# A separate issue order for each stage of an attention cycle, with other array halves for its scores

## The chip, the cores and the metric

The kernel runs on one core of one Trainium2 chip. The metric is the device time of one execution in microseconds (us). Three runs of the kernel before took 1853.1, 1853.3 and 1855.0 us; the median is 1853.3.

In the profile PE is TensorE's matmuls, PEld its weight loads, DVE is VectorE, ACT ScalarE, POOL GpSimd and SP the engine that issues most DMAs. Views of single instructions give start and duration in us from the span's start.

## The reference

Two branches work on the same input x of 2048 rows (tokens) by 640 features. A is attention with 32 heads of 20 features; B is a Fourier mixing. A gate per row blends them.

```python
g = sigmoid((x * gate_w).sum(-1, keepdims=True))
# A: q, k, v = x @ wqkv, split into 32 heads of 20
p = softmax(q @ k.T * 20 ** -0.5)          # per head, 2048 x 2048
a = concat_heads(p @ v) @ wo
# B: DFT along the features, then along the rows, real part
ar, ai = x @ hid_re.T, x @ hid_im.T        # 2048 x 640
b = seq_re @ ar - seq_im @ ai              # 2048 x 640
return g * a + (1 - g) * b
```

## The kernel before

**The attention's grain.** The 32 heads are 16 pairs; a pair is worked in two units of 1024 query columns, so there are 32 units. A unit has 32 steps: 16 tiles of 128 keys times 2 groups of 512 queries. One step is two "e" scores, one per head of the pair. An "e" is a matmul of 62 rows by 512 columns into a PSUM bank (line 1076) and an exponential on ScalarE that reads the bank (line 1082).

The maximum that the exponential needs is found ahead of time, by "m" scores: the same products with queries as the stationary side (line 194), each followed by a maximum over 512 columns on VectorE (line 196). They run 43 steps ahead of the "e" scores (LEAD). After a unit's last "m" the maxima are negated, split and turned, and go through DRAM into two more rows of the query operand, so that the later product comes out with the maximum subtracted.

**Array halves.** The two heads of a pair lie on rows 0 to 63 and 64 to 127 of their operands. A score therefore uses one half of the TensorE array, by rows: half 0 or half 1. In a step's two scores z = 0 comes first and z = 1 second, and the table FIRST says which of the two goes to which half: h = z, flipped where the table has a 1. The table has an entry for each of the four steps of a cycle and one row each for "e" and "m". All scores, "e" and "m" alike, take their banks in turn from the same five (`bank()`, line 142).

**The other branch as filler.** Branch B, with its sums of rows and columns combined so that fewer products are needed, is cut into pairs of matmuls: one on half 0 into bank yp0 and one on half 1 into bank yp1, 64 rows by 320 columns each. Pairs come from one long chain of generators: `hid_pair` (line 482, the DFT along the features), `dft_step` (line 779, along the rows) and `out_tile` (line 861, the output projection of finished rows). When a tile's last pair is issued, the reading of yp0 by ScalarE and of yp1 by VectorE is put into `extras`, with the step at which it falls due, and adds and stores are set for later steps.

**A cycle.** Everything is issued in one order written out by hand. A cycle is four steps, and a string says what is issued in it: "e" and "m" are scores, "F" is a place for pairs, and "B" is the burst. In the burst due extras run, and then the attention's second product (`av_step`, line 715; the matmuls of line 721) for the two key tiles whose exponentials are finished. These use all 128 rows, so neither half can work on scores or pairs meanwhile.

```python
ORDER = "emFemFFFFemFeFFmeFFemFFFmmFFmeeB"
LATE = "eeeeFFFFFFeeeEB"
FIRST = {"e": (0, 0, 1, 1), "m": (1, 1, 1, 1)}
```

There are 256 cycles. Cycles 0 to 55 are the hidden stage, with 15 pairs each; 56 to 223 the sequence stage, with 48 pairs in three cycles; 224 to 245 carry output tiles, 12 pairs each, in the same string ORDER; and from 246 on LATE is used. There the "m" scores have run out, and already in cycle 245 none is left. ORDER has 15 places. The list `goals` (lines 984 to 990) spreads a cycle's pairs over its places: with 16 pairs one place gets two, with 12 some places get none.

**What hangs on the order.** `score` (line 1055) issues a score and its reader; the first "e" of a step calls `begin`, which issues the DMAs set for that step, and the second calls `end`. `fill` (line 1000) issues pairs until the place's goal is reached. `burst` (line 1090) runs extras whose step has come. The steps at which extras, stores and loads fall due are counted from `now[0]`, the step whose "e" scores were begun last.

Of the kernel before, what the change touches and what calls it, by code (L numbers as in the profile page):

```python
# [32 lines left out]

ORDER = "emFemFFFFemFeFFmeFFemFFFmmFFmeeB"
LATE = "eeeeFFFFFFeeeEB"
FIRST = {"e": (0, 0, 1, 1), "m": (1, 1, 1, 1)}


LEAD = 43
# [49 lines left out]
def mix_kernel(ctx: ExitStack, tc: tile.TileContext, xa, xh, wqk, wb, wr, cdft, wo, out):  # L91
    nc = tc.nc
    pe, act, dve, pool, sp = nc.tensor, nc.scalar, nc.vector, nc.gpsimd, nc.sync
# [81 lines left out]

    mx, nms, ends = {}, {}, []
    rows_, done_tiles = [], []
    now, later = [-1], {}

    def at_step(i, fn):  # L180
        later.setdefault(i, []).append(fn)
# [302 lines left out]
    def hid_pair(u):  # L484
        n, hf, k = u // 8, u // 4 % 2, u % 4
        _, _, factor, targets = FEATURE[n]
        ps = [new_y(z)[:, :HE] for z in range(2)]
        fresh = [(th, ri, hf, k) not in seen for _, th, ri in targets]
        seen.update((th, ri, hf, k) for _, th, ri in targets)
        rows = [a_scr[ri, hf, th, k] for _, th, ri in targets]  # L490
        olds = []
        for (_, th, ri), new, row in zip(targets, fresh, rows):
            old = None
            if th == ri:
                old = acc(ri, hf, k)
            elif not new:
                old = slots.pop(0)
                slots.append(old)
                at_step(now[0] + 4, functools.partial(sp.dma_start, old, row))
            olds.append(old)  # L500
        done_ = 0
        for d in range(ND):
            for a, b in ((0, 0), (0, 1), (1, 0)):
                for z in range(2):
                    r = slice(64 * z, 64 * z + 64)
                    pe.matmul(ps[z], lefts[n][a][r, d, k * P : k * P + P], rights[2 * n + hf][r, b, d],  # L506
                              start=done_ == 0, stop=done_ == 3 * ND - 1)
                done_ += 1
                if done_ < 3 * ND:
                    yield  # L510
        direct = [i for i, ((_, th, ri), new) in enumerate(zip(targets, fresh)) if new and th == ri]
        m = olds[direct[0]] if direct else raw_tile()[:, : 2 * HE].rearrange("p (s c) -> p s c", s=2)

        def read():
            act.activation(m[:, 0], ps[0], AF.Copy, scale=factor)
            dve.tensor_scalar(m[:, 1], ps[1], factor, 1.0, op0=ALU.mult, op1=ALU.mult)  # L516

        def add(sign, old):
            pool.tensor_tensor(old, old, m, op=ALU.add if sign > 0 else ALU.subtract)  # L519

        extras.append((now[0], read))
        ends_ = {(th, ri): i for i, f in enumerate(FEATURE) for _, th, ri in f[3]}
        for (sign, th, ri), new, row, old in zip(targets, fresh, rows, olds):
            if not new:
                extras.append((now[0] + 3, functools.partial(add, sign, old)))
            if th != ri or ends_[th, ri] == n:
                at_step(now[0] + (4 if new else 11), functools.partial(sp.dma_start, row, m if new else old))
        yield

    step = 0  # L530
# [38 lines left out]
    for s in range(0, NS, 2):  # L569
# [6 lines left out]
        if 4 <= s <= 12:  # L576
            add, finish = make_set(*sets.pop(0), *(pair_tile().rearrange("p z c -> p (z c)")[:, : RW // 2] for _ in range(2)))
# [199 lines left out]
    outs, extras, made = {}, [], {}  # L777

    def dft_step(g):
        n, t, s = g // NS // HT, g // NS % HT, g % NS  # L780
        if s == 0:
            new_y(0), new_y(1)
            outs[n, t] = []
        if s % 8 == 0 and g // 8 + 3 < 2 * UNITS:
            cfin.append(load_c(g // 8 + 3))
        if s % 8 == 4 and cfin and 2 < g // 8 + 2 < 2 * UNITS:
            cfin.pop(0)()
        if s == 8:
            for _, th, hf in PRODUCTS[n][2]:
                tt = th * HT + t  # L790
                y = None
                if (tt, hf) in signs:
                    y = apool[0].tile([P, HE], F32, name="yt", bufs=4)
                    sp.dma_start(y, y_scr[tt, :, hf * HE : (hf + 1) * HE])
                outs[n, t].append(y)
        c = cparts[g // 8]
        cs = slice((s % 8) * P, (s % 8 + 1) * P)
        a = at[n % 2, s]
        for z, (cz, az) in enumerate(((0, 0), (0, 1), (1, 0))):
            for h in range(2):  # L800
                r = slice(64 * h, 64 * h + 64)
                pe.matmul(yp[h][:, :HE], c[r, cz, cs], a[r, az], start=s == 0 and z == 0, stop=s == NS - 1 and z == 2)  # L802
            if z < 2:
                yield
        w = g % (HT * NS) - 16
        if n + 1 == len(PRODUCTS) and w >= 0:
            d, r = divmod(w, 8)
            if r == 0 and d < ND:
                wos[d] = raw_tile()[:, :D]
                sp.dma_start(wos[d], wo[:, d])  # L810
            if r == 5 and d < ND:
                raw = wos.pop(d)
                for h in range(2):
                    wos[d, h] = a_tile(1, 2 * d + h)
                    split(wos[d, h][:, 0], wos[d, h][:, 1], raw[:, h * HE : (h + 1) * HE], pool, pool)
        if s == NS - 1:
            m = apool[0].tile([P, HE], F32, name="m", bufs=3)
            y0, y1 = yp[0][:, :HE], yp[1][:, :HE]

            def read():  # L820
                act.activation(m, y0, AF.Copy)
                dve.tensor_tensor(m, y1, m, op=ALU.add)

            extras.append((now[0], read))
            for out_, y in zip(PRODUCTS[n][2], outs.pop((n, t))):
                extras.append((now[0] + 5, functools.partial(finish_y, out_, t, m, y)))
        yield


# [31 lines left out]
    def out_tile(tt, hf):  # L861
        new_y(0), new_y(1)
        if hf == 0:
            k = tt - PRE[0]
            yo[tt] = f32(a_tile(1, 12 + k) if k < 4 else a_tile(0, k)).rearrange("p z c -> p (z c)")
            assert all(st[tt, h] == 0 for h in range(2))
            sp.dma_start(yo[tt], y_scr[tt])
        o = opre[tt]
        for d in range(ND - 1):
            for z, (oz, wz) in enumerate(((0, 0), (0, 1), (1, 0))):  # L870
                for h in range(2):
                    r = slice(64 * h, 64 * h + 64)
                    pe.matmul(yp[h][:, :HE], o[r, oz, d], wos[d, hf][r, wz], start=d == 0 and z == 0, stop=d == ND - 2 and z == 2)  # L873
                if (d, z) != (ND - 2, 2):
                    yield
        m = apool[0].tile([P, HE], F32, name="m", bufs=3)
        y0, y1 = yp[0][:, :HE], yp[1][:, :HE]
        g = gate[:, tt : tt + 1]

        def read():  # L880
            if now[0] < total - LEAD:
                act.activation(m, y0, AF.Copy, scale=g)
            else:
                dve.tensor_scalar(m, y0, g, 1.0, op0=ALU.mult, op1=ALU.mult)
            dve.scalar_tensor_tensor(m, y1, g, m, op0=ALU.mult, op1=ALU.add)  # L885

        def add():
            y = yo[tt][:, hf * HE : (hf + 1) * HE]
            pool.tensor_scalar(y, y, ngate[:, tt : tt + 1], float(signs[tt, hf]), op0=ALU.mult, op1=ALU.mult)
            pool.tensor_tensor(y, y, m, op=ALU.add)  # L890

        extras.append((now[0], read))
        extras.append((now[0] + 3, add))
        yield

    def finish_y(target, t, m, y):
# [63 lines left out]
    HID = 8 * len(FEATURE)  # L960
# [20 lines left out]
        at_tile += n  # L981
    assert cycles[-1][1] <= last + 1
    late = -(-(total - LEAD) // 4)
    at_goal = 0
    for c0, c1, count in cycles:
        for c in range(c0, c1):
            share = count * (c + 1 - c0) // (c1 - c0) - count * (c - c0) // (c1 - c0)
            places = (LATE if c >= late else ORDER).count("F")
            goals[c] = [at_goal + share * (f + 1) // places for f in range(places)]
            at_goal += share  # L990

# [63 lines left out]
    def score(kind):  # L1055
# [2 lines left out]
        heads[kind] += 1  # L1058
        i, z = divmod(x, 2)
        h = z  # L1060
        if kind == "m" or i <= 4 * late:
            h ^= FIRST[kind][(i - (LEAD if kind == "m" else 0) - 1) % 4]
        if kind == "m":
            s_mm(i, h)()
            if z:
# [44 lines left out]
        else:  # L1110
            score(kind)
    for c in range(total // 4):
        for kind in "e" * (c == late) + (LATE if c >= late else ORDER):
            if kind == "F":
                fill(c)
            elif kind == "B":
                burst(c)
            else:
                score(kind)
# [125 lines left out]
```

## Time and profile before

| | |
|---|---|
| median of three runs | 1853.3 us |
| the profiled execution's own time | 1854.3 us |
| its span, first to last instruction | 1852.5 us |
| mean granted TensorE clock | 0.999 |
| TensorE matmuls in flight | 99% of the span |
| weight loads / VectorE / ScalarE / GpSimd busy | 72% / 79% / 67% / 70% |
| hidden stage, cycles 1 to 55 | 345.6 us |
| sequence stage, 168 cycles | 1063.7 us |
| output stage, 21 cycles with "m" scores | 128.3 us |

A stage's time runs from the start of one burst to the start of another. The time of a cycle is the stage's time over its cycles. In the views that follow, a row of the busy time by stretches gives the stretch, its length, the busy time and number of instructions of each engine, the granted clock, the share of the DMA engines and GB/s. A row of the timeline gives start, duration, engine, line, operation, output and inputs, shape and how many instructions of one kind follow each other, and in brackets the idle time before it with what ended it.

### The profile page before, as it was taken

To read this page: it belongs to the slowest core of one execution; us is meant where nothing else is said; L and a number is where in the kernel's file an instruction comes from. 1 tells how busy PE (TensorE), PEld (TensorE's weight loads), DVE (VectorE), ACT (ScalarE), POOL (GpSimd) and SP (SyncE) were. 2 spreads that over 40 slices of the span, in tenths; PEclk is the share of its full clock that TensorE was granted. 3 is DMA by queue.
4 is the path that set the end of the run, shared out by engine and by line. 5 is a ranking of instruction groups with operands and counts; after the bars stand their busy time and mean duration, and the time that the engine had idled before them with its cause. 6 is when DMAs were issued, how large, how long until landed. Compare 5 with 4: busy or idle time off the path is not lost. (4 is left out here: it accounts for less than half of the span.)

```text
span 1852.5 us, 45906 instructions
## 1 busy us (share of the span) xinstructions
PE 1842.4 (99%) x17917; PEld 1339.8 (72%) x17917; DVE 1460.3 (79%) x2428; ACT 1237.0 (67%) x2378; POOL 1302.6 (70%) x1103
## 2 busy tenths in 40 slices
PE   9999999999999999999999999999999999999998
PEld 8988877677676677677677767767767767766666
DVE  4157489888888888888888888888888888889953
ACT  4233377777777677677766767667676767777785
POOL 1379635666678988556879999867889898734444
PEclk9999999999999999999999999999999999999999
DMA  7899874777666675536577686646585856542224
GB/s 236 203 312 360 291 212 142 224 217 210 222 215 203 193 224 157 145 101 177 184 203 240 171 254 191 199 123 181 156 222 185 233 163 187 154 105 76 64 56 155
DMA packets 195101, 349.63 MB, mean 189 GB/s; under 512 B 54095, under 2 KB 107471, under 8 KB 192835
## 3 DMA queue, kind: packets, MB, share of 16 engines
q1 hardware_dynamic: 193523, 340.63, 61.2%
q0 software_dynamic: 1360, 6.07, 1.5%
q8 instruction: 141, 2.31, 0.5%
q14 instruction: 77, 0.63, 0.1%
HBM read 257.79 MB, written 88.65 MB: 187 GB/s over the span
## 5 line engine op out<-in xcount | busy, mean ns | idle before, releaser
L196 DVE TENSOR_REDUCE mx<-ps 128x1 f32<-128x512 f32 x2048 | 1300.4, 686 | 209.7 <-PE ps L194 190.8
L1082 ACT ACTIVATE p<-ps 128x512 f32<-128x512 f32 x2048 | 1088.1, 598 | 424.5 <-PE ps L194 218.3
L194 PE MATMUL ps<-kst,qst 60*128 60x512 f32 x2048 | 776.5, 413 | 1.1 <-DMA qst<-qk_scr 0.8
L1076 PE MATMUL ps<-qst,kst 62*128 62x512 f32 x2048 | 695.5, 415 | 0.6 <-DMA qst<-m_scr 0.6
L802 PE MATMUL yp<-x,part 64*128 64x320 f32 x5376 | 644.8, 306 | 0.0
L802 PEld LDWEIGHTS yp<-x,part 64*128 64x128 f32 x5376 | 582.5, 186 | 7.6
L1076 PEld LDWEIGHTS ps<-qst,kst 62*128 62x128 f32 x2048 | 332.6, 184 | 223.6 <-DVE mx L196 128.9
L721 PE MATMUL av<-p,v 128*21 128x512 f32 x4096 | 492.5, 596 | 0.0
L194 PEld LDWEIGHTS ps<-kst,qst 60*128 60x128 f32 x2048 | 368.0, 184 | 13.3 <-issue 1.1
L133 POOL TENSOR_TENSOR part<-raw,part 128x1024 fp32r<-128x1024 f32 (+3 forms) x134 | 296.8, 2215 | 10.2
L721 PEld LDWEIGHTS av<-p,v 128*21 128x21 f32 x4096 | 95.3, 100 | 207.4 <-issue 206.5
L132 POOL CAST part<-raw 128x1024 fp32r<-128x1024 f32 (+2 forms) x127 | 125.0, 985 | 129.7 <-PE yp L802 93.3
L667 POOL TENSOR_TENSOR raw<-raw,raw 128x1024 f32<-128x1024 f32 x78 | 188.1, 2412 | 38.6 <-DMA raw<-in_cdft 23.1
L506 PE MATMUL yp<-wb,x 64*128 64x320 f32 x1680 | 207.6, 307 | 0.0
L506 PEld LDWEIGHTS yp<-wb,x 64*128 64x128 f32 x1680 | 179.7, 186 | 3.2 <-DVE x L516 0.2
L519 POOL TENSOR_TENSOR x<-x,raw 128x640 f32<-128x640 f32 x40 | 62.5, 1563 | 44.4 <-DVE raw L516 40.9
L133 POOL TENSOR_TENSOR x<-araw,x 128x320 fp32r<-128x320 f32 x96 | 83.8, 872 | 7.7
L873 PE MATMUL yp<-x,part 64*128 64x320 f32 x720 | 87.2, 308 | 0.0
L890 POOL TENSOR_TENSOR x<-x,m 128x320 f32<-128x320 f32 x30 | 26.2, 873 | 79.1 <-DVE m L885 68.4
L873 PEld LDWEIGHTS yp<-x,part 64*128 64x128 f32 x720 | 75.8, 185 | 2.6
L696 POOL TENSOR_TENSOR araw<-araw 128x320 f32<-128x320 f32 x80 | 69.9, 873 | 1.9 <-DMA araw<-a_scr 1.9
L366 PE MATMUL yp<-x,part 64*128 64x512 f32 x480 | 64.2, 397 | 1.8 <-ACT p L372 1.5
(111 smaller groups left out, 1369.5 us busy)
## 6 DMA issues: line engine op xcount, KB each, us to landing
raw<-in_cdft SPq DMA_DIRECT2D x188, 512.0 KB
araw<-a_scr SPq DMA_DIRECT2D x176, 160.0 KB
qk_scr<-p SPq DMA_DIRECT2D x40, 512.0 KB
w_scr<-wb SPq DMA_DIRECT2D x36, 400.0 KB
wb<-w_scr SPq DMA_DIRECT2D x9, 1600.0 KB
kst<-qk_scr SPq DMA_DIRECT2D x90, 160.0 KB
qst<-qk_scr SPq DMA_DIRECT2D x90, 160.0 KB
part<-in_xh SPq DMA_DIRECT2D x10, 1024.0 KB
```

What stands on the lines that cost most here:

```text
L132: e1.tensor_copy(dst1, src)
L133: e2.tensor_tensor(dst2, src, f32(dst1), op=ALU.subtract)
L194: pe.matmul(ps, q[b : b + KROWS, qt * P : (qt + 1) * P], k[b : b + KROWS, kc * 512 : (kc + 1) * 512], start=True, stop=True)
L196: return lambda: dve.tensor_reduce(mx[n][:, h, qt, kc : kc + 1], ps, axis=AX.X, op=ALU.max)
L506: pe.matmul(ps[z], lefts[n][a][r, d, k * P : k * P + P], rights[2 * n + hf][r, b, d], start=done_ == 0, stop=done_ == 3 * ND - 1)
L667: pool.tensor_tensor(raws[0], raws[0], raws[1], op=ALU.add if PRODUCTS[n][0][1][0] > 0 else ALU.subtract)
L696: pool.tensor_tensor(raws[0], raws[0], raws[1], op=ALU.add if PRODUCTS[n][1][1][0] > 0 else ALU.subtract)
L721: pe.matmul(av[32 * j : 32 * j + DH + 1, :], v[:, kt, h * (DH + 1) : (h + 1) * (DH + 1)], pp[qc][:, h, :], start=kt == 0, stop=kt == NS - 1)
L802: pe.matmul(yp[h][:, :HE], c[r, cz, cs], a[r, az], start=s == 0 and z == 0, stop=s == NS - 1 and z == 2)
L873: pe.matmul(yp[h][:, :HE], o[r, oz, d], wos[d, hf][r, wz], start=d == 0 and z == 0, stop=d == ND - 2 and z == 2)
L1076: pe.matmul(pt, k[b : b + KROWS + 2, kt * P : (kt + 1) * P], q[b : b + KROWS + 2, qc * 512 : (qc + 1) * 512], start=True, stop=True)
L1082: act.activation(pts[n, kt, qc][:, h], pt, AF.Exp, scale=float(DH) ** -0.5)
```

## The change

Each of the three stages gets a string and a pair of half tables of its own. The sequence stage's string has 16 places, the output stage's 12, and the hidden stage's keeps 15, so that each place gets exactly one pair. The number of scores, pairs and bursts in a cycle stays the same. The late stage keeps its string, and its tables hold zeros, which is what its scores had before.

In the new strings the last "F" of a cycle comes after the cycle's last step has begun. The new function `ended` caps the step from which due times are counted at the step before it, so that reads, adds and stores are due at the steps they had.

```diff
-ORDER = "emFemFFFFemFeFFmeFFemFFFmmFFmeeB"
-LATE = "eeeeFFFFFFeeeEB"
-FIRST = {"e": (0, 0, 1, 1), "m": (1, 1, 1, 1)}
+HIDDEN = "emeFFmeFFFmFeFmeFFmFFeFFeFFmemmB", {"e": (0, 1, 1, 1), "m": (1, 0, 1, 0)}
+SEQUENCE = "ememFFeFFFFmeFFmeFmFFFeFFemFFmemB", {"e": (1, 0, 1, 0), "m": (0, 1, 1, 1)}
+OUTPUT = "ememeFFFmFeFmFeFmeFFmFemFFemB", {"e": (1, 0, 0, 0), "m": (0, 0, 1, 1)}
+LATE = "eeeeFFFFFFeeeEB", {"e": (0, 0, 0, 0), "m": (0, 0, 0, 0)}
...
-    now, later = [-1], {}
+    now, at_cycle, later = [-1], [0], {}
+
+    def ended():
+        return min(now[0], 4 * at_cycle[0] + 3)
...
-        extras.append((now[0], read))
+        extras.append((ended(), read))
...
-                extras.append((now[0] + 3, functools.partial(add, sign, old)))
+                extras.append((ended() + 3, functools.partial(add, sign, old)))
             if th != ri or ends_[th, ri] == n:
-                at_step(now[0] + (4 if new else 11), functools.partial(sp.dma_start, row, m if new else old))
+                at_step(ended() + (4 if new else 11), functools.partial(sp.dma_start, row, m if new else old))
...
+    def plan(c):
+        return LATE if c >= late else OUTPUT if c >= edge[-1] else SEQUENCE if c >= HID else HIDDEN
+
     at_goal = 0
     for c0, c1, count in cycles:
         for c in range(c0, c1):
             share = count * (c + 1 - c0) // (c1 - c0) - count * (c - c0) // (c1 - c0)
-            places = (LATE if c >= late else ORDER).count("F")
+            places = plan(c)[0].count("F")
...
         h = z
-        if kind == "m" or i <= 4 * late:
-            h ^= FIRST[kind][(i - (LEAD if kind == "m" else 0) - 1) % 4]
+        h ^= plan(at_cycle[0])[1][kind][(i - (LEAD if kind == "m" else 0) - 1) % 4]
...
     for c in range(total // 4):
-        for kind in "e" * (c == late) + (LATE if c >= late else ORDER):
+        at_cycle[0] = c
+        for kind in "e" * (c == late) + plan(c)[0]:
```

The same replacement of `now[0]` by `ended()` is made where `dft_step` and `out_tile` append their extras.

More of the change, by code (lines that the diff above doesn't have):

```diff
@@ L822, in read @@
                 dve.tensor_tensor(m, y1, m, op=ALU.add)
-            extras.append((now[0], read))
+            extras.append((ended(), read))
             for out_, y in zip(PRODUCTS[n][2], outs.pop((n, t))):
-                extras.append((now[0] + 5, functools.partial(finish_y, out_, t, m, y)))
+                extras.append((ended() + 5, functools.partial(finish_y, out_, t, m, y)))
         yield
@@ L890, in add @@
             pool.tensor_tensor(y, y, m, op=ALU.add)
-        extras.append((now[0], read))
-        extras.append((now[0] + 3, add))
+        extras.append((ended(), read))
+        extras.append((ended() + 3, add))
         yield
```

## The prediction

> **What bounds the kernel now.** I read the page's head first, then the busy time by stage, then one cycle of each stage instruction by instruction, and last what the two readers of the scores (ScalarE's exponential, VectorE's maximum) wait for.
>
> ```profile
> span 1852.5 us, 45906 instructions
> PE 1842.4 (99%) x17917; PEld 1339.8 (72%) x17917; DVE 1460.3 (79%) x2428; ACT 1237.0 (67%) x2378; POOL 1302.6 (70%) x1103
> ```
>
> TensorE has work in flight all the time, and the two readers are far from full; but a busy matmul can also be one that stands and waits. So the cycle has to be taken apart. The attention's own products (line 721) count the cycles, 16 instructions to each:
>
> ```profile
> 237.50:583.07 345.57, 105.73 (x880) 20.30 (x880) 1.00 0.69 206
> 583.07:1646.80 1063.73, 322.92 (x2690) 62.06 (x2690) 1.00 0.62 181
> 1646.80:1775.10 128.30, 40.31 (x336) 7.79 (x336) 1.00 0.29 78
> ```
>
> That is 55 cycles of the hidden stage at 6.28 us (880/16; 345.57/55), 168 of the sequence stage at 6.33, and 21 of the output stage at 6.11, on a granted clock of 1.00. The rest (start, the 11 late cycles, the end) is 315 us and is not touched.
>
> One ordinary sequence cycle on TensorE (start, duration, line; L1076 is an "e", L194 an "m", L802 a pair's matmul, L721 the burst):
>
> ```profile
> 900.96 0.49 PE L1076 MATMUL ps<-qst,kst 62*128 62x512 f32 x1
> 900.96 0.49 PE L194 MATMUL ps<-kst,qst 60*128 60x512 f32 x1
> 901.29 0.31 PE L802 MATMUL yp<-x,part 64*128 64x320 f32 x2
> 901.44 0.39 PE L194 MATMUL ps<-kst,qst 60*128 60x512 f32 x1
> 901.44 0.39 PE L1076 MATMUL ps<-qst,kst 62*128 62x512 f32 x1
> 901.68 0.74 PE L802 MATMUL yp<-x,part 64*128 64x320 f32 x8
> 902.26 0.39 PE L1076 MATMUL ps<-qst,kst 62*128 62x512 f32 x1
> 902.26 0.44 PE L194 MATMUL ps<-kst,qst 60*128 60x512 f32 x1
> ...
> 905.04 0.44 PE L1076 MATMUL ps<-qst,kst 62*128 62x512 f32 x2
> 905.41 0.63 PE L721 MATMUL av<-p,v 128*21 128x512 f32 x4
> ...
> 907.26 0.50 PE L1076 MATMUL ps<-qst,kst 62*128 62x512 f32 x1
> ```
>
> Two matmuls on different array halves run side by side. On one half a score keeps the next matmul off for 0.235 us (901.44 to 901.68), a pair's matmul for 0.145 (four pairs from 901.68 to 902.26). A half has 8 scores and 16 pairs: 8 x 0.235 + 16 x 0.145 = 4.20 us. Around it stand 1.95 us from the burst's start to the first score's stream (905.41 to 907.26, and 0.10 more, as the first record lasts 0.49 where 0.39 is usual) and 0.33 from the last score's start (905.04 + 0.44 - 0.39 = 905.09) to the burst. The floor of a cycle is 1.95 + 4.20 - 0.235 + 0.33 = 6.245 us. This cycle took 6.30 (900.96 to 907.26): only 0.055 is waiting. The floor with 15 pairs is 6.10, with 12 it is 5.665.
>
> What the waiting is shows at 902.26: that "m" is 0.05 too long. It is the cycle's sixth score, and there are five banks, so it takes the first score's bank, once that has been read:
>
> ```profile
> 901.55 0.60 ACT L1082 ACTIVATE p<-ps 128x512 f32<-128x512 f32 x1 [1.24 <-PE ps L194]
> 902.20 0.18 PEld L194 LDWEIGHTS ps<-kst,qst 60*128 60x128 f32 x1
> ```
>
> The exponential ends at 902.15, the weight load goes at 902.20 (0.05 later) and the stream starts at 902.31 (0.11 later). **So a cycle is bound by its halves, plus the lateness of score k+5 behind the reader of score k.** The other stages have more of it:
>
> ```profile
> 502.40 0.49 PE L1076 MATMUL ps<-qst,kst 62*128 62x512 f32 x1
> 508.62 0.49 PE L1076 MATMUL ps<-qst,kst 62*128 62x512 f32 x1
> ...
> 1691.55 0.50 PE L1076 MATMUL ps<-qst,kst 62*128 62x512 f32 x1
> 1692.80 0.18 PEld L194 LDWEIGHTS ps<-kst,qst 60*128 60x128 f32 x1
> 1697.67 0.49 PE L1076 MATMUL ps<-qst,kst 62*128 62x512 f32 x1
> ```
>
> A hidden cycle of 6.22 is 0.12 over its floor, an output cycle of 6.12 is 0.45 over. In the output stage empty places bring the sixth score forward, and its load waits until 1692.80 for the same first exponential.
>
> **How the two halves keep step** decides the change, and the old trace shows it in a cycle where one half ran far ahead:
>
> ```profile
> 1296.26 0.40 PE L1076 MATMUL ps<-qst,kst 62*128 62x512 f32 x1
> 1296.32 0.44 PE L194 MATMUL ps<-kst,qst 60*128 60x512 f32 x1
> 1296.50 0.55 PE L802 MATMUL yp<-x,part 64*128 64x320 f32 x4
> ...
> 1296.65 0.41 PE L802 MATMUL yp<-x,part 64*128 64x320 f32 x2
> ...
> 1296.31 0.69 DVE L196 TENSOR_REDUCE mx<-ps 128x1 f32<-128x512 f32 x1 [0.28 <-PE ps L194]
> 1297.03 0.69 DVE L196 TENSOR_REDUCE mx<-ps 128x1 f32<-128x512 f32 x1
> ```
>
> The list has "e F F m" here. The "m", on half 0, starts 0.06 after the "e" of half 1, and the two half-1 matmuls of the pairs between them start only at 1296.50 and 1296.65: a half starts ahead of what stands before it on the other half. But the maximum of this "m", done at 1296.76, starts at 1297.03. The maximum before it started at 1296.31 and lasts 0.69, so VectorE had nothing to do from 1297.00 at the latest. 1297.03 is 0.07 after the end of the last half-1 pair matmul ahead of it (1296.65 and a usual 0.31: 1296.96). **Starts run ahead, reports don't**: a score is told to its reader when all that precedes it in the list is done. By the Trainium skill ("TensorE: Matmul & The Clock Gate", Part 3) matmuls keep program order in start and in end; the trace bears out the end and not the start.
>
> **The change, part by part.** No instruction is added or taken away: 16 scores, 15, 16 or 12 pairs and one burst per cycle, as before.
>
> *Sequence stage, 168 cycles.* With the new tables the list reads (digit: the half) e1 m0 e0 m1 FF e0 FFFF m1 e1 FF m0 e1 F m1 FFF e0 FF e0 m0 FF m1 e1 m0. Laid out with 0.235 and 0.145 from the first stream:
> - sixth score (m1): half 1 reaches it at 2 x 0.235 + 6 x 0.145 = 1.34; its bank allows 902.31 - 901.06 = 1.25. The old lateness of 0.05 is gone.
> - eleventh score (e0): half 0 reaches it after 4 scores and 12 pairs, at 2.68. Half 1 has had two scores more by then. Its third matmul of the FFF ahead of this e0 starts after 6 scores and 11 pairs, 1.41 + 1.595 = 3.005, and ends 0.306 later (row below) at 3.31. The report comes with it: exponential 3.38 to 3.98 (0.07, 0.60), load 4.03, stream 4.14.
> - sixteenth score (m0), which takes that bank: half 0 reaches it after 7 scores and 16 pairs, at 3.965. It is 0.175 late, and nothing but the burst is behind it.
>
> ```profile
> L802 PE MATMUL yp<-x,part 64*128 64x320 f32 x5376 | 644.8, 306 | 0.0
> ```
>
> The cycle becomes 1.95 + 4.14 + 0.33 = 6.42 for 6.30. I take +0.115: **168 x 0.115 = +19.3 us**. Its bounds: -0.055 (to the floor) if nothing is late, and +0.35 (the fourth rival).
>
> *Hidden stage, 55 cycles.* e0 m1 e1 FF m0 e1 FFF m0 F e0 F m1 e1 FF m1 FF e0 FF e1 FF m0 e0 m0 m1. The eleventh score (e0) streams at 2.535; the half-1 pair matmul ahead of it starts after 6 scores and 10 pairs, 2.86, and ends 3.17. Exponential 3.24 to 3.84, load 3.89, stream of the sixteenth score (m1) 4.00; half 1 reaches it at 7 x 0.235 + 15 x 0.145 = 3.82. Cycle: 1.95 + 4.00 + 0.33 = 6.28, against 6.22 in the row and 6.28 in the mean, which holds disturbed cycles too. I take +0.045: **+2.5 us**; bounds -0.12 and +0.06 a cycle.
>
> *Output stage, 21 cycles.* e1 m0 e0 m1 e0 FFF m0 ...: the sixth score is reached at 3 x 0.235 + 3 x 0.145 = 1.14, before at 2 x 0.235 + 4 x 0.145 = 1.05 (em em FFFF e m, the first place being empty); the bank allows 1.25. The lateness falls by 0.09. Afterwards half 1 leads by two scores for one pair, while the wait for that sixth load holds both halves, and then no half leads by more than one: **21 x -0.09 = -1.9 us**; bounds 0 and -0.45 (to the floor).
>
> *Due times, reads, queues.* The last pairs of a cycle now come after its last step has begun; the new cap on the step number keeps reads, adds and stores at their old steps. Steps' DMA issues on SP, and the loads that pairs issue, move by less than a cycle against each other. They are issued ahead, and this is all that TensorE waited for a DMA in the sequence stage:
>
> ```profile
> PE ps L1076 <- DMA qst<-m_scr: 0.6, 1, 0.6
> ```
>
> I cost this at 0, bounds -0.6 and +3 (a few such waits more). The late order is the same string, with halves as they were.
>
> Sum: 19.3 + 2.5 - 1.9 = **+19.9 us**. The profiled execution took 1854.3 us for a span of 1852.5, the median is 1853.3; the difference carries to the median: 1853.3 + 19.9 = **1873 us**.
>
> **Rivals.**
> 1. *No score is told late.* If a score's own end is enough for its reader, all of 3.38 to 4.14 moves forward by 0.3 and no last score waits. Sequence to its floor (168 x -0.055 = -9.2), hidden to its floor and 0.05, since its sixth score stays late (6.15 for 6.22, 55 x -0.07 = -3.9), output -1.9: 1838 us. For it: the late start is one reading of pipelined records, whose ends are modelled. Against it: the maximum at 1297.03.
> 2. *The late score is absorbed.* A chain shorter by 0.12 than laid out (report, exponential, load) makes the sequence stage neutral: with hidden and output about 1854. Against it: its pieces are rows.
> 3. *Starts in list order too.* Then a score that stands alone, or beside one of its own half, holds both halves up. The old list has 9 such rounds, the new ones 12, 13 and 12: 168 x 3 x 0.235 + 55 x 4 x 0.235 + 21 x 3 x 0.235 = 185, so 2038 us. The starts at 1296.32 and 1296.50 speak against it. The sentence of the Trainium skill told above, taken whole, is this case.
> 4. *Only half 0 may run far ahead.* The new sequence list lets half 1 lead by a score (e0 FFFF). If half 1's pairs must wait there for half 0's, all that half 1 does later, and with it the report of the eleventh score, comes 0.235 later: 0.115 + 0.235 = 0.35 a cycle, 168 x 0.35 + 2.5 - 1.9 = 59, so 1912 us. Half 1 has been ahead, but little: here its pair matmul behind an "e" of half 1 is the first of the two, by 0.02.
>
> ```profile
> 440.31 0.39 PE L1076 MATMUL ps<-qst,kst 62*128 62x512 f32 x1
> 440.32 0.40 PE L194 MATMUL ps<-kst,qst 60*128 60x512 f32 x1
> 440.54 0.33 PE L506 MATMUL yp<-wb,x 64*128 64x320 f32 x2
> ```
>
> **How the numbers follow.** Forecast 0.73 (own range 1860 to 1886: the chain 0.05 shorter or longer, 8 us, and 4 of queues); first rival 0.11, second 0.07, third 0.02, fourth 0.07. What a measurement of this kernel can tell from no change is about 0.2%, 3.7 us. Faster is the first rival, 0.11; same the second, 0.07; slower the rest, 0.82. The range runs from 1844, between the second and the first rival, to 1888.
>
> **What would show it.** In the new trace: sequence cycles near 6.41, hidden near 6.28, output near 6.02; the eleventh score's exponential starting about 0.3 after that matmul's own end; the load of a cycle's last "m" alone and late, with one half empty before the burst. Sequence cycles near 6.245 would refute the report in list order; cycles over 6.6, half 1's lead.

## The result, and the profile after

The changed kernel takes 1875.0 us (median of six runs, 1872.5 to 1880.1), the kernel before 1853.2 in its six: 1.0121 times the time, 95% interval 1.0109 to 1.0133. The forecast was 1873 us, slower, in a range of 1844 to 1888.

The profiled execution happens to be the slowest of the six (1880.1 us). Its stages, by the attention's own products (stretch, length, busy and number of TensorE's instructions, of weight loads, clock, DMA share, GB/s):

```profile
238.50:593.00 354.50, 105.73 (x880) 20.31 (x880) 0.99 0.67 201
593.00:1674.10 1081.10, 322.92 (x2688) 62.09 (x2688) 1.00 0.60 178
1674.10:1801.00 126.90, 40.33 (x336) 7.81 (x336) 1.00 0.31 81
```

Against the kernel before the hidden stage gains 8.9 us in length (354.5 for 345.6), the sequence stage 17.4 (1081.1 for 1063.7), and the output stage loses 1.4 (126.9 for 128.3). Most of the 8.9 belongs to this one execution: a single wait of TensorE for a load, after which the granted clock stood at half for 6.8 us, made one cycle 12.1 us long. This is the wait, in the table of who waited for whom (engine and line, what it waited for: us in total, times, longest), and the stretch behind it, with the clock of 0.50 third from the end:

```profile
PE ps L198 <- DMA qst<-qk_scr: 2.8, 1, 2.8
```

```profile
572.56:579.39 6.83, 6.00 (x38) 5.87 (x40) 3.60 (x6) 2.50 (x5) 6.61 (x6) 0.50 0.94 281
```

With that cycle at the usual 6.3 the hidden stage is some 3 us longer than before.

One sequence cycle of the changed kernel, first the rows of TensorE, then ScalarE's and the weight load's. The line numbers have moved: L1083 is an "e", L198 an "m", L806 a pair's matmul, L725 the burst, L1089 the exponential.

```profile
878.03 0.50 PE L1083 MATMUL ps<-qst,kst 62*128 62x512 f32 x1
...
880.83 0.40 PE L1083 MATMUL ps<-qst,kst 62*128 62x512 f32 x1
...
881.16 0.45 PE L806 MATMUL yp<-x,part 64*128 64x320 f32 x3
...
882.13 0.40 PE L1083 MATMUL ps<-qst,kst 62*128 62x512 f32 x1
882.18 0.49 PE L198 MATMUL ps<-kst,qst 60*128 60x512 f32 x1
882.61 1.91 PE L725 MATMUL av<-p,v 128*21 128x512 f32 x16
884.45 0.50 PE L1083 MATMUL ps<-qst,kst 62*128 62x512 f32 x1
...
881.53 0.60 ACT L1089 ACTIVATE p<-ps 128x512 f32<-128x512 f32 x1 [0.20 <-PE yp L806]
...
882.18 0.18 PEld L198 LDWEIGHTS ps<-kst,qst 60*128 60x128 f32 x1
```

The cycle is 6.42 us (878.03 to 884.45). Its eleventh score is the "e" at 880.83, done at 881.23. Its exponential starts only at 881.53, after 0.20 of idle time that the profile itself puts down to a pair's matmul: the last one of half 1 ahead of that score in the list, begun at 881.16 and done at 881.47. It ends at 882.13. The load of the sixteenth score, which takes the same bank, goes at 882.18, and the burst, for which nothing else is missing by the rows, at 882.61.

That this happens in nearly every cycle shows in the table of waits, first of the kernel before, then of the changed one:

```profile
ACT p L1082 <- PE yp L802: 2.0, 3, 1.5
```

```profile
ACT p L1089 <- PE yp L806: 32.8, 167, 0.2
```

Three waits of an exponential for a pair's matmul have become 167, 0.2 us each, in a stage of 168 cycles.

### The profile page after: what moved, and what is told of

It reads as the page before. It is cut to its first block, busy times and chain, and to the rows that moved or that the text cites. A ratio compares the mean times of both kernels' runs of the same rounds, so it can differ in the third digit from the quotient of the medians.

```text
span 1878.3 us, 45838 instructions
## 1 busy us (share of the span) xinstructions
PE 1863.5 (99%) x17917; PEld 1350.2 (72%) x17917; DVE 1447.8 (77%) x2428; ACT 1253.3 (67%) x2378; POOL 1303.4 (69%) x1103
## 5 line engine op out<-in xcount | busy, mean ns | idle before, releaser
L1089 ACT ACTIVATE p<-ps 128x512 f32<-128x512 f32 x2048 | 1104.5, 599 | 415.1 <-PE ps L198 317.5
L1083 PE MATMUL ps<-qst,kst 62*128 62x512 f32 x2048 | 769.8, 408 | 0.0
L198 PE MATMUL ps<-kst,qst 60*128 60x512 f32 x2048 | 756.9, 420 | 4.5 <-DMA qst<-qk_scr 2.8
L806 PE MATMUL yp<-x,part 64*128 64x320 f32 x5376 | 620.7, 305 | 0.0
L806 PEld LDWEIGHTS yp<-x,part 64*128 64x128 f32 x5376 | 581.6, 185 | 14.8
L1083 PEld LDWEIGHTS ps<-qst,kst 62*128 62x128 f32 x2048 | 354.3, 185 | 220.6 <-issue 173.7
L725 PE MATMUL av<-p,v 128*21 128x512 f32 x4096 | 492.5, 596 | 0.0
L198 PEld LDWEIGHTS ps<-kst,qst 60*128 60x128 f32 x2048 | 355.8, 185 | 26.4 <-issue 3.1
L725 PEld LDWEIGHTS av<-p,v 128*21 128x21 f32 x4096 | 95.4, 100 | 201.9 <-issue 201.0
L510 PE MATMUL yp<-wb,x 64*128 64x320 f32 x1680 | 214.6, 310 | 0.9 <-DVE x L520 0.9
L510 PEld LDWEIGHTS yp<-wb,x 64*128 64x128 f32 x1680 | 194.7, 188 | 5.3 <-DVE x L520 1.8
L877 PE MATMUL yp<-x,part 64*128 64x320 f32 x720 | 90.0, 312 | 0.0
```

The lines of the kernel that those rows point to most:

```text
L198: pe.matmul(ps, q[b : b + KROWS, qt * P : (qt + 1) * P], k[b : b + KROWS, kc * 512 : (kc + 1) * 512], start=True, stop=True)
L725: pe.matmul(av[32 * j : 32 * j + DH + 1, :], v[:, kt, h * (DH + 1) : (h + 1) * (DH + 1)], pp[qc][:, h, :], start=kt == 0, stop=kt == NS - 1)
L1083: pe.matmul(pt, k[b : b + KROWS + 2, kt * P : (kt + 1) * P], q[b : b + KROWS + 2, qc * 512 : (qc + 1) * 512], start=True, stop=True)
L1089: act.activation(pts[n, kt, qc][:, h], pt, AF.Exp, scale=float(DH) ** -0.5)
```

## The experiments

**The report moved, and nothing else.** If the list order of reports is the cause, it must be possible to cure the loss without touching what either half does. A place "G" issues only the half-0 matmul of its pair and keeps the half-1 matmul back until the next "e" is issued; a "g" keeps the half-0 matmul back.

```diff
-HIDDEN = "emeFFmeFFFmFeFmeFFmFFeFFeFFmemmB", ...
-SEQUENCE = "ememFFeFFFFmeFFmeFmFFFeFFemFFmemB", ...
+HIDDEN = "emeFFmeFFFmFeFmeFFmGGeFFeFFmemmB", ...
+SEQUENCE = "ememFFeFFFFmeFFmeFmGGGeFFemFFmemB", ...
+    def pair_mm(h, *args, **kw):
+        mm = functools.partial(pe.matmul, *args, **kw)
+        parked.append(mm) if park[0] == h else mm()
...
                 score(kind)
+                while kind == "e" and parked:
+                    parked.pop(0)()
```

> The changed kernel, with only the list order of some matmuls moved: in the sequence stage the half-1 matmuls of the FFF ahead of the eleventh score, in the hidden stage those of the FF ahead of it, are issued right behind that score. Each half's own sequence of matmuls, all banks and all halves stay as they are. Theory (a score is told only when all before it in the list is done): the eleventh score is told 0.3 us earlier and the sixteenth is no longer late; sequence cycles 6.25 (from 6.43), hidden cycles 6.15 (from 6.30), output unchanged at 6.04; 1838 us. Rival A (the lead of one half costs by itself, by starved halves or clashing starts): no cycle changes, 1875 us. Rival B (the new places or bank turns hurt): no cycle changes, 1875 us.

It took 1843.3 us, 0.9952 of the kernel before (95% interval 0.9938 to 0.9965): the whole loss is gone and more, though 5 us less than the 1838 expected. Its stages, and its cycle around the eleventh score:

```profile
237.20:580.10 342.90, 105.70 (x880) 20.26 (x880) 1.00 0.68 208
580.10:1635.70 1055.60, 322.93 (x2688) 62.08 (x2688) 1.00 0.61 182
1635.70:1762.60 126.90, 40.33 (x336) 7.80 (x336) 1.00 0.29 81
```

```profile
858.40 0.50 PE L1088 MATMUL ps<-qst,kst 62*128 62x512 f32 x1
...
861.20 0.39 PE L1088 MATMUL ps<-qst,kst 62*128 62x512 f32 x1
861.26 0.46 PE L1136 MATMUL yp<-x,part 64*128 64x320 f32 x2
...
861.56 0.30 PE L1136 MATMUL yp<-x,part 64*128 64x320 f32 x1
...
864.70 0.49 PE L1088 MATMUL ps<-qst,kst 62*128 62x512 f32 x1
...
861.63 0.60 ACT L1094 ACTIVATE p<-ps 128x512 f32<-128x512 f32 x1
```

The half-1 matmuls (now line 1136) still run after the "e" has begun (861.20); but its exponential starts at 861.63, 0.04 after the score's own end (861.59). Nothing but the report moved: counted from the first stream (858.50), the "e" starts at 2.70 and the third half-1 matmul at 3.06; in the changed kernel's cycle it was 2.70 and 3.03. The cycle is 6.30 here (858.40 to 864.70) and 6.28 on average (1055.6 / 168); I had expected 6.25. The hidden stage came to 6.23 (342.9 / 55) for 6.15, with a median cycle of 6.17. Rivals A and B, by which nothing would change, fall.

**The same with the other sign.** The strings have "FFF" and "gg" ahead of the eleventh score in the sequence stage (hidden: "FF" and "gg"), taken from the two pairs behind it.

```diff
+HIDDEN = "emeFFmeFFFmFeFmeFFmFFggeeFFmemmB", ...
+SEQUENCE = "ememFFeFFFFmeFFmeFmFFFggeemFFmemB", ...
```

> The same with the opposite sign: two pairs that stand behind the eleventh score are issued ahead of it with their half-1 matmuls only, and their half-0 matmuls right behind it; each half's own sequence stays as it is. Theory: the eleventh score waits for two more half-1 matmuls, 2 x 0.145 = 0.29 us, and the cycle grows by as much: sequence 6.71, hidden 6.58; 1940 us. Rivals A and B: no cycle changes, 1875 us.

1938.8 us in one run. The stages, the wait, and the rows around the eleventh score (L491 is a pair's matmul issued in its place, L1136 one that was kept back):

```profile
237.90:601.40 363.50, 105.73 (x880) 20.31 (x880) 1.00 0.65 196
601.40:1732.80 1131.40, 322.90 (x2690) 62.01 (x2690) 1.00 0.57 170
1732.80:1859.70 126.90, 40.31 (x336) 7.79 (x336) 1.00 0.29 81
```

```profile
ACT p L1094 <- PE yp L1136: 106.4, 224, 0.5
```

```profile
906.26 0.50 PE L1088 MATMUL ps<-qst,kst 62*128 62x512 f32 x1
...
908.93 0.49 PE L491 MATMUL yp<-x,part 64*128 64x320 f32 x2
909.27 0.50 PE L1088 MATMUL ps<-qst,kst 62*128 62x512 f32 x1
...
909.70 0.31 PE L491 MATMUL yp<-x,part 64*128 64x320 f32 x1
...
910.08 0.60 ACT L1094 ACTIVATE p<-ps 128x512 f32<-128x512 f32 x1 [0.49 <-PE yp L1136]
...
910.73 0.18 PEld L198 LDWEIGHTS ps<-kst,qst 60*128 60x128 f32 x1 [0.17 <-ACT p L1094]
```

The eleventh score is the "e" at 909.27, done at 909.77. Its exponential starts at 910.08, 0.07 after the end of the last half-1 matmul ahead of it (909.70 and 0.31). The profile names line 1136 instead, which here issues the half-0 matmuls behind the score: it goes by what ended about then, and the second of those ends at 910.06.

Sequence cycles came to 6.73 (1131.4 / 168) and hidden ones to 6.61 (363.5 / 55), near what was laid out (6.71 and 6.58). The three kernels have the same matmuls on each half in the same sequence, and differ in how many half-1 matmuls stand in the list ahead of one score: 6.28, 6.44 (1081.1 / 168) and 6.73 us a cycle. From the second to the third, two matmuls of 0.145 more make 0.30.

But in this run more than the report moved. The score itself streams 3.01 us after the first stream (909.37 and 906.36, each 0.10 behind its record), and not at 2.70, although its half is free from 909.08 (its last pair matmul started at 908.93, and 0.145). Over the sequence stage its record starts 2.88 to 2.91 us after the first stream, where it is 2.69 to 2.76 in the other two kernels. With three half-1 matmuls ahead of it in the list the score starts ahead of all of them; with five it starts when two of them have started. So a half's lead was bounded here; by what was not tried. By the prices of the layout, half 0 would then reach the sixteenth score at 3.01 + 3 x 0.235 + 4 x 0.145 = 4.30 with no late report at all; it streams at 4.48 (910.73 and 0.11), released by the exponential. So the report binds here too, but the late start alone would have made some 0.14 of the 0.30 (an estimate, against 4.16 in the changed kernel). The first experiment is the clean one.

**Other tables for the same strings.**

```diff
-HIDDEN = "emeFFmeFFFmFeFmeFFmFFeFFeFFmemmB", {"e": (0, 1, 1, 1), "m": (1, 0, 1, 0)}
-SEQUENCE = "ememFFeFFFFmeFFmeFmFFFeFFemFFmemB", {"e": (1, 0, 1, 0), "m": (0, 1, 1, 1)}
+HIDDEN = "emeFFmeFFFmFeFmeFFmFFeFFeFFmemmB", {"e": (0, 0, 1, 1), "m": (1, 0, 0, 0)}
+SEQUENCE = "ememFFeFFFFmeFFmeFmFFFeFFemFFmemB", {"e": (0, 0, 0, 0), "m": (1, 1, 1, 1)}
```

> The changed kernel's strings with other half tables for the hidden and the sequence stage, sequence e (0,0,0,0), m (1,1,1,1), hidden e (0,0,1,1), m (1,0,0,0). Laid out as in the prediction, the lag is then on the half of the eleventh score itself, which streams 0.24 later, and the sixteenth score stays 0.14 late in the sequence stage; in the hidden stage nothing is told late: sequence 6.38, hidden 6.24, 1863 us. Rival C (the tables alone are the fault and the new strings are good): at or below the kernel before in both stages, 6.30 or less and 6.25 or less, 1853 us or less.

1868.7 us in one run; sequence 6.41 a cycle, hidden 6.33:

```profile
238.10:586.10 348.00, 105.71 (x880) 20.30 (x880) 1.00 0.68 205
586.10:1662.80 1076.70, 322.91 (x2688) 62.02 (x2688) 1.00 0.61 179
```

```profile
902.09 0.49 PE L1083 MATMUL ps<-qst,kst 62*128 62x512 f32 x1
...
905.12 0.39 PE L1083 MATMUL ps<-qst,kst 62*128 62x512 f32 x1
...
905.55 0.60 ACT L1089 ACTIVATE p<-ps 128x512 f32<-128x512 f32 x1 [0.17 <-PE ps L1083]
```

The eleventh score streams 2.93 us after the first stream (905.12 and 902.19), 0.23 later than in the changed kernel, and its exponential follows its own end (905.51). In the sequence stage the tables alone are not the fault (rival C falls there): with these two pairs of tables the eleventh score of this string comes late either by its report or by itself. The hidden stage's mean holds one cycle of 7.6 us and seven above 6.48; its median cycle is 6.26, near the 6.24 expected, and rival C is open there.

**The sequence stage alone put back.**

```diff
-SEQUENCE = "ememFFeFFFFmeFFmeFmFFFeFFemFFmemB", {"e": (1, 0, 1, 0), "m": (0, 1, 1, 1)}
+SEQUENCE = "emFemFFFFemFeFFmeFFemFFFmmFFmeeB", {"e": (0, 0, 1, 1), "m": (1, 1, 1, 1)}
```

> The changed kernel with the old string and the old tables in the sequence stage alone; hidden and output stage as changed. Theory: the sequence stage carries nearly all of the loss, so its 168 cycles are back at 1064 us, hidden stays 2 us above the kernel before, output 1.5 below; 1854 us. Rival (the loss is a sum over all stages, or of the loads whose place moved): 1860 us or more.

1856.0 us, 1.0017 of the kernel before (1.0008 to 1.0027).

```profile
236.90:585.70 348.80, 105.72 (x880) 20.31 (x880) 1.00 0.68 204
585.70:1647.20 1061.50, 322.91 (x2688) 62.03 (x2688) 1.00 0.62 181
1647.20:1774.10 126.90, 40.33 (x336) 7.82 (x336) 1.00 0.30 81
```

The hidden stage is 3.2 us longer than before and the output stage 1.4 shorter. What the change did to these two stages costs some 1.5 to 5 us in the timed runs (the interval); the sequence stage's order costs the rest, about 19 (1875.0 - 1856.0). The rival, 1860 us or more, falls. The sequence stage has the order of before here and took 1061.5 us for 1063.7, so a difference of 2 us between the stages of two profiled executions tells nothing.

**Strings chosen by the rule.** If the rule is right, an order in which no score is told late must be faster than both the kernel before and the changed one.

```diff
+HIDDEN = "emFemFFeFFmeFFmFeFFmeFFFmFFmemeB", {"e": (0, 0, 0, 1), "m": (1, 1, 1, 0)}
+SEQUENCE = "emFemFFeFFFmeFFmeFFmFeFFFmFmFeemB", {"e": (0, 1, 0, 0), "m": (1, 0, 1, 1)}
```

> Other strings and tables for the hidden and the sequence stage, chosen by the rule that no score should be told late: hidden emFemFFeFFmeFFmFeFFmeFFFmFFmemeB with e (0,0,0,1), m (1,1,1,0); sequence emFemFFeFFFmeFFmeFFmFeFFFmFmFeemB with e (0,1,0,0), m (1,0,1,1); output as changed. Every place has one pair, as in the change. Theory: no score but the hidden stage's sixth is late, so sequence cycles come to their floor, 6.25, hidden to 6.15, output 6.04; 1838 us. Rival B (one pair to a place, or 16 places, hurts whatever the order): sequence stays above 6.30, 1853 us or more.

1842.7 us, 0.9939 (0.9926 to 0.9951).

```profile
237.40:578.30 340.90, 105.72 (x880) 20.31 (x880) 1.00 0.70 209
578.30:1636.50 1058.20, 322.97 (x2692) 62.13 (x2696) 1.00 0.61 182
```

Sequence 6.30 and hidden 6.20 on average, with median cycles of 6.28 and 6.16. This run's rival B (one pair to a place, or 16 places, hurts whatever the order) expected 1853 us or more and falls by the time, though the mean cycle lies at its mark of 6.30. Yet of the 13.7 us that the sequence stage was to gain (1063.7 to 168 x 6.25) only 5.5 came. Four cycles of 6.44 to 7.14 us hold 2.0 of the rest; why they are long was not tried. Nor is every score told in time:

```profile
ACT p L1089 <- PE yp L806: 8.1, 20, 0.4
```

These 20 are the last exponentials of their cycles, and most of those cycles take 6.27 us, no more than the others.

**The two cures together.** Hidden stage as in the kernel just told, sequence stage with the list of the first experiment.

> The hidden stage's string and tables of even_orders, the sequence stage's list of reports_early, the output stage as changed. Theory: the stages add, so hidden 341 us, sequence 1056, output 127: 1841 us, below both kernels, and within 3 us of even_orders and reports_early, since all three stand near the floor of the sequence stage. Rival (what remains above the floor is the list order of the sequence stage): no forecast of its own but a sequence stage below 1050.

1839.9 us, 0.9933 (0.9920 to 0.9945): the lowest median of this study, though its time cannot be told from that of the two kernels it is made of. Hidden 341.3, sequence 1055.6 and output 127.1 us are what was laid out (341, 1056, 127), and the rival's sequence stage below 1050 did not come.

```profile
236.80:578.10 341.30, 105.73 (x880) 20.31 (x880) 1.00 0.69 209
578.10:1633.70 1055.60, 322.96 (x2692) 62.11 (x2694) 1.00 0.62 182
1633.70:1760.80 127.10, 40.29 (x336) 7.78 (x336) 1.00 0.30 81
```

## Why the prediction was right

**Reports in list order** was the step on which the sign hung. The first experiment, which moves nothing but a report, shows it, and the second, in which the score's start moves too, bears it out. The chain laid out for the eleventh score stands in the trace to within 0.03 us. From the first stream (878.03 and 0.10, so 878.13) the "e" streams at 2.70 (laid out: 2.68), the half-1 matmul starts at 3.03 (3.005), the exponential at 3.40 (3.38), and the last "m", loaded at 882.18 and streaming 0.11 later, at 4.16 (4.14).

**Sequence stage**, +19.3: measured +17.4 in the profiled executions. The cycle came out as said (6.42; the mean is 6.44). What was mis-sized is the term's base: I took 6.30 for a cycle of before, one ordinary cycle, and the mean was 6.33. From burst to burst the median cycle went from 6.30 to 6.43, by 0.13 and so by more than the 0.115 forecast; but the kernel before has five cycles of 6.54 to 7.31 us in this stage and the changed one none above 6.50, and so the mean moved by only 0.10.

**Hidden stage**, +2.5: +3.2 where the same order was profiled without the long wait. The 0.045 a cycle was picked between 0 and 0.06, not worked out; the median cycle went from 6.25 to 6.30. **Output stage**, -1.9: -1.2 to -1.5 in the profiles. No run tests by itself that this gain is the sixth score's.

**Due times, reads, queues**, 0 with a bound of +3: in the profiled execution of the changed kernel alone a wait of 2.8 us for a load and the half clock behind it cost 5.8 us, more than the bound. The medians differ by 21.8 us where the stages, that cycle left aside, give 17.4 + 3.2 - 1.4 = 19.2. Of the other 2.6 the profiles show 1.0 ahead of the first counted burst (238.5 for 237.5, a start that varies from 236.8 to 238.5 among all profiles). The rest is that the profiled execution of before took 1.1 more than its median (1854.3 for 1853.2), and that of the changed kernel, less the 5.8, 0.7 less than its own (1874.3 for 1875.0). That 1873 and 1875.0 lie so close is in part luck: the sequence term was 2 us too large, and this remainder was not forecast.

**The rivals.** The first (no score told late) falls with the first two experiments. The second (absorbed, 1854 us) falls with the 167 waits and the time. The third (starts in list order) would have made 2038 us, and the rows below speak against it too. The fourth (half 1 can't run ahead) is refuted by the changed kernel's own cycle:

```profile
878.90 0.39 PE L1083 MATMUL ps<-qst,kst 62*128 62x512 f32 x1
879.04 0.31 PE L806 MATMUL yp<-x,part 64*128 64x320 f32 x1
```

The first row is the lone "e" of half 0, which holds that half until 879.13; the pair's matmul that starts at 879.04 is half 1's, ahead of its partner, which stands before it in the list. Either half may lead, here half 1 and at 1296.32 in the kernel before half 0.

The Trainium skill's sentence ("TensorE: Matmul & The Clock Gate", Part 3) that matmuls keep program order in start and end holds here for what the readers are told (881.53 behind 881.47), not for the starts (879.04 ahead of 879.13).

## What to carry to other kernels

Where two array halves run different work, as in this kernel, lay out each half's own sequence and then ask for every result which matmul ahead of it in the list finishes last: its reader is told when that one is done. A half that leads gains nothing for its readers, and its lead was bounded when five of the other half's matmuls stood ahead in the list. Put a result ahead of the lagging half's matmuls in the list, which cost nothing here, or keep the lead under the slack that the rotation of banks leaves.

## What the runs showed that was not expected

The order of issue alone, with each half's work unchanged, moved the kernel from 1843.3 to 1938.8 us, a twentieth of its time.

The floor of a sequence cycle, 6.245 us by the rows, was not reached: cycles stood at 6.28 (median 6.27) in the first experiment, where hardly an exponential is left that waits for a pair's matmul. Maxima on VectorE still do, and whether they cost anything was not tried:

```profile
DVE mx L200 <- PE yp L491: 19.1, 76, 0.5
...
ACT p L1094 <- PE yp L491: 0.3, 1, 0.3
```

The floor may itself be too low. The 0.145 of a pair is from one stretch of four pairs; in the changed kernel's cycle 6 scores and 11 pairs took 3.03 where the layout has 3.005. The same excess on 16 pairs would be 0.036 us, an estimate from these figures, which is about what is missing. (The 0.33 in the floor is 0.32 by its own rows, 905.09 to 905.41.)
